# A set-attention block with a gated feed-forward layer: in the last batch, from slot 12 on, products 1024 wide with two value tiles of two banks and three gate tiles of one bank, stage 2's scores copied aside first

## The chip, the cores and the metric

The kernel runs on one core of one Trainium2 chip. The metric is the time of one execution on the device, in microseconds (us); the time before is the median of three executions. TensorE (PE in the profile) multiplies matrices and writes PSUM, which has eight banks of 512 float32 values per partition; VectorE (DVE) and ScalarE (ACT) read PSUM, GpSimd (POOL) does not; SyncE (SP) issues most of the transfers.

## The reference

There are four batches of 12416 tokens of 128 channels, 32 inducing vectors, and a feed-forward layer of width 1536.

```python
def mab(q, kv):
    s = scale * (q @ kv.transpose(0, 2, 1))
    s = s - s.max(-1, keepdims=True)
    a = np.exp(s)
    a /= a.sum(-1, keepdims=True) + 1e-09
    return a @ kv
h = mab(I, x)          # stage 1: 32 inducing vectors attend to the tokens
x = mab(x, h)          # stage 2: every token attends to the 32 rows of h
gate = 1.0 / (1.0 + np.exp(-(x @ w_gate)))
val = x @ w_val
out = gate * val @ w_out
```

## The kernel before

Stage 2's result is never built. The attention weights of a token have only 32 entries, so the kernel multiplies `h` by the two weight matrices once per batch (`hwt`, the tile named `hw`) and obtains value and gate of a token directly from its 32 weights (`a2r`). A matmul for this is 32 rows deep and 512 columns (tokens) wide; which quarter of TensorE's rows it takes follows from the column group `j` and from whether it is a gate (rows 0 or 32) or a value (rows 64 or 96).

The work of the feed-forward layer is cut into *blocks* of 512 tokens, 24 blocks per batch, and one last block of 128 tokens of each batch: 97 blocks. A block has 12 column groups `j` of 128 hidden units (`NJ` = 12). These 12 are done in *steps*: a step of two groups (1024 columns for VectorE and ScalarE), then one of one group (512 columns), and so on, so that a block has four pairs of steps, 776 steps in all. For a step `t`,

- `hidden_mm(st, "v")` fills the value tile and `hidden_mm(st, "g")` the gate tile, by TensorE (line 1012),
- `gate(t)` takes tanh of half the gate from PSUM to `t16`, by ScalarE (line 1031),
- `product(t)` computes (tanh + 1) x value from PSUM to `u16`, by VectorE (line 1044),
- `project` multiplies `u16` by `w_out` and adds up in the accumulator bank `acc`, four matmuls of 128 x 128 per column group, by TensorE (line 1075); at a block's end ScalarE copies the accumulator, halved, to `o32` (line 1093) and SyncE stores it.

PSUM is full: the value and the gate tile of a pair have two banks each (`v2`, `g2`), those of a single one each (`v1`, `g1`), the accumulator has one (`acc`), and one (`m`) serves all else: scores of both stages, sums, the making of `hwt`. Each tag has one buffer, so a tile is filled again only once its last reader is done.

The order of the work is written by hand, and every engine's queue runs in it. The main loop calls, for each step, `product(t)` (which issues the value fills of `t` and the gate fills of `t + 2`), `gate(t + 2)`, and every second step a slot of other work (`beside`) and then `project` with up to three or four column groups. Two steps make one slot. The other work is planned by slot in the dictionary `plan`: `plan_stage2(b, c, score, take, weigh, ...)` puts the scores of 16 tokens' columns at the slots `score` and `score + 1` (TensorE, line 611, eight matmuls each into bank `m`), their copy to `sc` at `take` (ScalarE, line 645), the subtraction of the maximum by GpSimd (`lower`), the exponential at `weigh` (ScalarE, line 671), and sums, scaling and a transposing transfer after it. For the last batch the groups' scores lie at slots 4, 20, 36 and 56 after its first step (`o`).

Of the kernel before, what the change touches and what calls it, by code (L numbers as in the profile page):

```python
# [9 lines left out]
F32 = mybir.dt.float32  # L10
# [7 lines left out]
P = 128  # L18
GC = 16
# [7 lines left out]
def kernel(  # L27
# [34 lines left out]

    ps = ctx.enter_context(tc.tile_pool(name="ps", bufs=1, space=bass.MemoryType.PSUM))

    xv = x.rearrange("b (p j) c -> b p j c", p=P)
    ov = out.rearrange("(b p j) c -> b p j c", b=B, p=P)
# [648 lines left out]
        for j in range(n):  # L717
            a2[(b, c + j)] = (a2r, j)

    def plan_stage2(b, c, score, take, weigh, far=None, soon=False, lag=None):  # L720
# [6 lines left out]
        def room():  # L727
            st["sc"] = s2p.tile([P, GC + NLO, m], F32, tag="sc", name="sc", bufs=1)
# [265 lines left out]
    for i in range(len(blocks)):  # L994
        for j in range(0, NJ, 3):
            steps.append(dict(block=i, j0=j, cnt=2))
            steps.append(dict(block=i, j0=j + 2, cnt=1))
    NST = len(steps)

    def hidden_mm(st, what, halves=False):  # L1000
        pt = ps.tile([P, st["cnt"], 512], F32, tag=f"{what}{st['cnt']}", name=f"{what}_ps")
        pieces, col = [], 0
        for b, c, nb in blocks[st["block"]]:
            pieces += [(k, b, c, nb, col) for k in range(st["cnt"])]
            col += nb * P
        if not halves and st["block"] < len(blocks) - 1:
            pieces.sort(key=lambda p: p[0])
        for k, b, c, nb, col in pieces:
            j = st["j0"] + k
            r = 32 * (j % 2 + (2 if what == "v" else 0))  # L1010
            a2r, o = a2[(b, c)]
            st[what + "end"] = nc.tensor.matmul(  # L1012
                pt[:, k, col : col + nb * P],
                hw[b][r : r + 32, j // 2, :],
                a2r[r : r + 32, o : o + nb, :].rearrange("p j t -> p (j t)"),
                start=True,
                stop=True,
            )
        st[what] = pt

    def gate_fill(t):
        if t < NST:
            hidden_mm(steps[t], "g", t == 0)

    def gate(t):
        if t < NST:
            st = steps[t]
            st["t"] = tp.tile([P, st["cnt"], 512], F16, tag=f"t{st['cnt']}", name="t16")
            cuts = [0, 512] if t else [0, 256, 512]
            for c, e in zip(cuts, cuts[1:]):  # L1030
                st["tanh"] = nc.scalar.activation(  # L1031
                    out=st["t"][:, :, c:e], in_=st["g"][:, :, c:e], func=AF.Tanh, scale=0.5
                )

    def product(t):
        st = steps[t]
        hidden_mm(st, "v")
        if t == 0:
            keep_on(3, "acc")
        gate_fill(t + 2)  # L1040
        st["u"] = up.tile([P, st["cnt"], 512], F16, tag=f"u{st['cnt']}", name="u16")
        cuts = [0, 512] if 0 < t < NST - 1 else [0, 256, 512]
        for c, e in zip(cuts, cuts[1:]):
            u = nc.vector.scalar_tensor_tensor(  # L1044
                out=st["u"][:, :, c:e],
                in0=st["t"][:, :, c:e],
                scalar=1.0,
                in1=st["v"][:, :, c:e],
                op0=ALU.add,
                op1=ALU.mult,  # L1050
            )
            if t == 0 and c == 0:
                turn_b()
        if st["cnt"] == 2 and 4 <= t < NST - 2:

            tc.declare_no_dep(u.ins, st["tanh"].ins, reason="the gate fill of t + 2 waits for it")
            tc.add_manual_dep(
                u.ins, steps[t + 2]["gend"].ins.name, AFTER, reason="tanh, gate fill, product"
            )

    acc = [None]
# [3 lines left out]
    def project(upto, now, room):  # L1065
        while queue and queue[-1][0] < upto and room > 0:
            t, k = queue.pop()
            st = steps[t]
            j = st["j0"] + k
            if j == 0:  # L1070
                acc[0] = [ps.tile([P, BC, C], F32, tag="acc", name="acc_ps")]
                if st["block"] == len(blocks) - 1:
                    acc[0].append(ps.tile([P, BC, C], F32, tag="m", name="acc_ps"))
            for i in range(BC):
                nc.tensor.matmul(  # L1075
                    acc[0][(i // 2) % len(acc[0])][:, i, :],
                    st["u"][:, k, ts(i, P)],
                    wo16[:, NI * (j % 2) + j // 2, :],
                    start=(j == 0 and i in ((0, 2) if len(acc[0]) > 1 else (0,))),
                    stop=(j == NJ - 1),  # L1080
                    skip_group_check=True,
                )
            room -= 1
            if t == NST - 1:
                o32 = op.tile([P, BC, C], F32, tag="o32")
                nc.scalar.mul(out=o32[:, 0:2], in_=acc[0][0][:, 0:2], mul=0.5)
                nc.scalar.dma_start(ov0[:, 0, 0:2, :], o32[:, 0:2])
                nc.vector.tensor_scalar_mul(out=o32[:, 2:4], in0=acc[0][1][:, 2:4], scalar1=0.5)
                nc.sync.dma_start(ov0[:, 0, 2:4, :], o32[:, 2:4])
            elif j == NJ - 1:  # L1090
                block = blocks[st["block"]]
                o32 = op.tile([P, BC, C], F32, tag="o32")
                nc.scalar.mul(out=o32[:], in_=acc[0][0][:], mul=0.5)  # L1093
                b, c, nb = block[0]
                nc.sync.dma_start(ov[b, :, c : c + BC, :], o32[:])
                if now < NST:
                    return


    base = [first_step[(b, 0)] // 2 for b in range(B)]  # L1100
    for b in range(B):
# [6 lines left out]
        for s in range(3 if b == 0 else 2, NG - 1):  # L1108
            k = o + 16 * s - 28
            if b == 0 and s == 4:  # L1110
                k += 1
                plan_stage2(b, groups[s][0], k, k + 1, k + 13)
                continue
            lag = k + 4 if b and more and s == 3 else None
            plan_stage2(b, groups[s][0], k, k + 2, k + (14 if more else 10), lag=lag)
        late = 2 if more and b else 0
        plan_stage2(b, groups[NG - 1][0], o + 56, o + 58, o + 66, far=o + 52 + late)
        if not more:
            continue
        if b == 0:  # L1120
            parts = {
                2: (23, (29, 29, 29)),
# [98 lines left out]
```

## Time and profile before

| | |
|---|---|
| median of 3 executions | 716.75 us (716.66 to 716.96) |
| the profiled execution | 717.17 us |
| its span, first to last instruction | 715.1 us |
| granted TensorE clock | 1.00 |
| VectorE busy | 697.7 us (98%) |
| ScalarE busy | 674.2 us (94%) |
| TensorE busy | 647.6 us (91%) |
| GpSimd busy | 446.7 us (62%) |

A row of the profile names line, engine, operation, tile written <- tiles read, partitions x elements, count, and behind the bar the busy time in us, the mean of one in ns and the idle time ahead of it. A timeline's row begins with its start and its length in us; neighbours of one kind are drawn into one row (`x12`). For a matmul, 32\*128 or 128\*128 is its rows times columns of the array. Rows of one engine may overlap: the next instruction starts before the one ahead of it has delivered.

### The profile page before, as it was taken

The page shows a single profiled execution, that of the slowest core. Times are in us where ns is not written, and L with a number is a line of the kernel's source. Part 1 is how long each engine was busy: PE and PEld are TensorE (multiplying, and loading weights), DVE is VectorE, ACT ScalarE, POOL GpSimd, SP SyncE. Part 2 cuts the span into 40 slices and gives each one's busy share as a digit, 9 for nine tenths or more (in the row PEclk, how much of TensorE's full clock was granted, in tenths as well). Part 3 has the DMA queues.
Part 4 walks back from the last instruction along what each step waited for, and adds up shares of the span by engine and source line. Part 5 has one row for each costly group of instructions (what it writes and reads, how often), then busy time and mean ns, then how long its engine had stood idle before and what let it go on. Part 6 is the DMA issues. An engine that isn't in the chain of part 4 may idle for free.

```text
span 715.1 us, 21664 instructions
## 1 busy us (share of the span) xinstructions
PE 647.6 (91%) x8475; PEld 393.0 (55%) x8475; DVE 697.7 (98%) x850; ACT 674.2 (94%) x1018; POOL 446.7 (62%) x780
## 2 busy tenths in 40 slices
PE   7999899998999999999999989999989889898887
PEld 4555455555555555555555556555555555555555
DVE  4899999999999999999999999999999999999998
ACT  4799999999999999999999999999999999999996
POOL 4568863887558978668656887587737546535100
PEclk9999999999999999999999999999999999999999
DMA  8979864253583264255485132221222123121211
GB/s 172 176 134 181 144 133 95 75 120 87 111 162 77 63 119 107 58 118 109 92 154 107 53 76 77 57 64 46 62 76 60 46 75 61 45 61 46 67 40 47
DMA packets 117111, 65.24 MB, mean 91 GB/s; under 512 B 100208, under 2 KB 101392, under 8 KB 117008
## 3 DMA queue, kind: packets, MB, share of 16 engines
q1 hardware_dynamic: 112320, 49.83, 30.8%
q0 software_dynamic: 4416, 13.90, 10.9%
q8 instruction: 66, 1.08, 0.6%
q14 instruction: 37, 0.30, 0.1%
q10 hardware_dynamic: 272, 0.13, 0.1%
HBM read 27.80 MB, written 25.43 MB: 74 GB/s over the span
## 4 chain that ended last, share of the span: by engine, by line
DVE 48%; issue 20%; PE 17%; ACT 12%; DMA 2%; DVEq 1%; POOL 0%; ACTq 0%; POOLq 0%
DVE u L1044 46%; ACT t L1031 11%; PE acc_ps L1075 8%; PE v_ps L1012 6%; DMA xn<-in_x_dram 2%; PE hp_ps L283 1%; DVE nm L235 1%; DVEq L1044 1%; PE g_ps L1012 1%; POOL xn L82 0%; ACT a1T L248 0%; ACT hwt L470 0%; PE s_ps L223 0%; PE aT_ps L261 0%; PE s_ps L611 0%
## 5 line engine op out<-in xcount | busy, mean ns | idle before, releaser
L1044 DVE SCALAR_TENSOR_TENSOR u<-t,v_ps 128x512 f16<-128x512 f16 (+1 forms) x778 | 674.9, 945 | 1.1 <-ACT t L1031 0.6
L1031 ACT ACTIVATE t<-g_ps 128x512 f16<-128x512 f32 (+1 forms) x777 | 592.3, 820 | 20.6 <-ACT t L1031 12.5
L1012 PE MATMUL v_ps<-a2r,hwt 32*128 32x512 f16 (+1 forms) x1188 | 293.5, 371 | 55.3 <-DVE u L1044 53.9
L1075 PE MATMUL acc_ps<-wo,u 128*128 128x128 f16 x4656 | 327.4, 220 | 0.1
L1075 PEld LDWEIGHTS <-u 128*128 128x128 f16 x4656 | 261.0, 98 | 88.4 <-issue 87.5
L1012 PE MATMUL g_ps<-a2r,hwt 32*128 32x512 f16 (+1 forms) x1188 | 296.6, 377 | 0.0
L1012 PEld LDWEIGHTS <-hwt 32*128 32x128 f16 x2424 | 92.6, 91 | 185.9 <-issue 140.4
L701 POOL TENSOR_TENSOR a2n<-e,rs 128x2048 f16<-128x2048 f16 (+3 forms) x25 | 86.8, 3474 | 5.0 <-DVE rs L690 2.1
L679 POOL TENSOR_TENSOR sum<-e 128x256 f32<-128x256 f16 (+1 forms) x23 | 15.4, 670 | 97.5 <-ACT e L671 97.5
L440 POOL TENSOR_TENSOR near<-sme,minus 128x16 f32<-128x16 f32 (+1 forms) x22 | 65.2, 2963 | 1.6
L1093 ACT ACTIVATE o<-acc_ps 128x512 f32<-128x512 f32 x96 | 58.2, 606 | 0.0
L655 POOL TENSOR_TENSOR rise<-sc 128x256 f32<-128x256 f32 (+1 forms) x22 | 16.2, 738 | 43.4 <-ACT sc L645 43.3
L656 POOL TENSOR_SCALAR rise<-rise 128x256 f32<-128x256 f32 (+6 forms) x110 | 30.1, 273 | 9.6
L659 POOL TENSOR_TENSOR top<-top,rise 128x128 f32<-128x128 f32 (+3 forms) x88 | 28.3, 321 | 7.3
L679 POOL TENSOR_TENSOR sum<-sum 128x128 f32<-128x128 f32 (+3 forms) x92 | 28.3, 307 | 7.2
L655 POOL TENSOR_TENSOR rise<-top 128x128 f32<-128x128 f32 (+3 forms) x88 | 27.2, 309 | 6.9
L662 POOL TENSOR_TENSOR sc<-sc,top 128x512 f32<-128x512 f32 (+1 forms) x22 | 23.9, 1085 | 1.7
L611 PEld LDWEIGHTS <-xT 128*128 128x128 f16 x388 | 13.0, 96 | 11.7 <-issue 11.3
L82 POOL DMA_DIRECT2D xn<-in_x_dram x25 | 14.9, 602 | 6.5 <-DMA xn<-in_x_dram 5.6
L611 PE MATMUL s_ps<-hT,xT 128*128 128x32 f16 x388 | 18.1, 178 | 0.1
L659 POOL TENSOR_TENSOR top<-sc,rise 128x256 f32<-128x256 f32 (+1 forms) x22 | 16.2, 738 | 1.8
L362 POOL TENSOR_TENSOR xT<-xT 128x512 f32<-128x512 f32 (+2 forms) x13 | 12.4, 957 | 4.2 <-ACT xT L345 3.6
(160 smaller groups left out, 281.9 us busy)
## 6 DMA issues: line engine op xcount, KB each, us to landing
out_dram<-o SPq DMA_DIRECT2D x96, 256.0 KB, 2.2
xn<-in_x_dram POOLq DMA_DIRECT2D x19, 512.0 KB, 7.9
xn<-in_x_dram POOLq DMA_DIRECT2D x4, 544.0 KB, 6.2
a2r<-a2n SPq DMA_TRANSPOSE x29, 4.4
xT<-xn SPq DMA_TRANSPOSE x27, 4.3
xn<-in_x_dram POOLq DMA_DIRECT2D x1, 384.0 KB, 15.1
wg<-in_moe_w_gate_dram POOLq DMA_DIRECT2D x1, 384.0 KB, 16.5
wv<-in_moe_w_val_dram POOLq DMA_DIRECT2D x1, 384.0 KB, 16.6
```

The lines of the kernel that those rows point to most:

```text
L440: nc.gpsimd.tensor_tensor(out=near, in0=x, in1=minus, op=ALU.pow)
L611: nc.tensor.matmul(s2[:, j, :], xT[b][:, c + j, :], hT16[b][:], start=(j == 0), stop=whole and j == j1 - 1, skip_group_check=True,)
L655: nc.gpsimd.tensor_tensor(out=r, in0=far, in1=near, op=ALU.subtract)
L656: nc.gpsimd.tensor_scalar(out=r, in0=r, scalar1=BIG, scalar2=0.0, op0=ALU.min, op1=ALU.max)
L659: nc.gpsimd.tensor_tensor(out=top[:, 0:n, 0:w], in0=near, in1=r, op=ALU.add)
L679: nc.gpsimd.tensor_tensor(out=d[:, 0:n, :], in0=src[:, :, 0:w], in1=src[:, :, w : 2 * w], op=ALU.add)
L701: eng.tensor_tensor(out=a2n[:, 0:n, :, :], in0=e.unsqueeze(2).to_broadcast((P, n, 4, m)), in1=rs.unsqueeze(2).unsqueeze(3).to_broadcast((P ...
L1012: st[what + "end"] = nc.tensor.matmul(pt[:, k, col : col + nb * P], hw[b][r : r + 32, j // 2, :], a2r[r : r + 32, o : o + nb, :].rearrange ...
L1031: st["tanh"] = nc.scalar.activation(out=st["t"][:, :, c:e], in_=st["g"][:, :, c:e], func=AF.Tanh, scale=0.5)
L1044: u = nc.vector.scalar_tensor_tensor(out=st["u"][:, :, c:e], in0=st["t"][:, :, c:e], scalar=1.0, in1=st["v"][:, :, c:e], op0=ALU.add, op1= ...
L1075: nc.tensor.matmul(acc[0][(i // 2) % len(acc[0])][:, i, :], st["u"][:, k, ts(i, P)], wo16[:, NI * (j % 2) + j // 2, :], start=(j == 0 and ...
L1093: nc.scalar.mul(out=o32[:], in_=acc[0][0][:], mul=0.5)
```

## The change

The first 600 steps stay as they are, up to slot 12 of the last batch (`T0`). From there on, 22 blocks, the tags `g2`, `g1`, `v1` and `m` are closed, and their five banks are given out anew: a second value tile of two banks (`vw`, beside `v2`) and three gate tiles of one bank (`gw0`, `gw1`, `gw2`). A block then has six steps of two column groups, whose products are all 1024 wide, with value tiles `v2` and `vw` in turn; the gates are filled and put through tanh one column group at a time (`single_fill`, `single_gate`), into a ring of 24 places in the token tile of the batch before (`ring_t`).

Since bank `m` is gone, stage 2's scores of the last four groups of the last batch are computed before slot 12 (at `o - 8`, `o`, `o + 4`, `o + 8`) and copied into the transposed token tile of the batch before; GpSimd's part and all behind it keep their slots (`low`, `weigh`). The loop after `T0` issues per step the product, then twice a column group's projection, with a gate fill and a tanh between; behind a block's store one projection place stays empty.

Matmul work on TensorE around one pair of steps before, within the last batch (`hwt` is the stationary tile of a fill, `u` of a projection):

```order
L1012 LDWEIGHTS hwt
L1012 MATMUL v_ps<-a2r,hwt 128x512
...
L1012 MATMUL g_ps<-a2r,hwt 128x512
L1075 LDWEIGHTS u_14247
L1075 MATMUL acc_ps<-wo_109,u_14247 128x128
...
L1075 LDWEIGHTS u_14255
L1075 MATMUL acc_ps<-wo_109,u_14255 128x128
...
L1012 LDWEIGHTS hwt
L1012 MATMUL v_ps<-a2r,hwt 128x512
```

The left-out rows repeat these: behind the fills of value and gate stand eight projections of a pair and four of a single, and then the fills of the next pair and single, six matmuls, with nothing between them. Now one step of 1024 on TensorE:

```order
L1044 MATMUL v_ps<-a2r,hwt 128x512
...
L1044 MATMUL g_ps<-a2r,hwt 128x512
L1127 LDWEIGHTS u_14175
L1127 MATMUL acc_ps<-wo_112,u_14175 128x128
...
L1044 LDWEIGHTS hwt
L1044 MATMUL g_ps<-a2r,hwt 128x512
L1127 LDWEIGHTS u_14175
L1127 MATMUL acc_ps<-wo_112,u_14175 128x128
...
L1044 MATMUL v_ps<-a2r,hwt 128x512
```

Two value fills and one gate fill stand ahead of four projections, then one gate fill alone and four projections more, then the next step's value fills. Fills stand between projections twice per 1024 columns, where before they did so once per 1536. On ScalarE, one block before and behind it the next:

```order
L1093 ACTIVATE o_14199<-acc_ps 128x512
L1031 ACTIVATE t_14210<-g_ps 128x1024
L1031 ACTIVATE t_14226<-g_ps 128x512
...
L1093 ACTIVATE o_14331<-acc_ps 128x512
L1031 ACTIVATE t_14342<-g_ps 128x1024
```

And now (`xn` is the token tile that holds the ring, `xT` the one that holds the scores):

```order
L1145 ACTIVATE o_12841<-acc_ps 128x512
L1067 ACTIVATE xn_1758<-g_ps 128x512 x7
L684 ACTIVATE e<-xT_3926 128x512
L1067 ACTIVATE xn_1758<-g_ps 128x512 x5
L1145 ACTIVATE o_12973<-acc_ps 128x512
```

Between two output copies stood four tanh of 1024 and four of 512; now there are twelve of 512, and a stage 2 exponential in one of four blocks.

The diff, cut to its core:

```diff
+    class Banks:
+        pools = {}
+        def open(self, stack, name, *tags):
+            pool = stack.enter_context(tc.tile_pool(name=name, bufs=1, space=bass.MemoryType.PSUM))
+            self.pools.update((tag, pool) for tag in tags)
+    ps.open(ctx, "ps", "v2", "acc")
+    ps.open(narrow, "psn", "g2", "g1", "v1", "m")
...
         def room():
+            if low is not None:
+                c0 = (c - NLO) // GC * 9
+                st["sc"] = (
+                    xT[b - 1][:, c0 : c0 + 9, :]
...
-            at(take if lag is None else lag, lower, late=lag is None)
+            at(low or take if lag is None else lag, lower, late=lag is None)
...
+    gates = steps
+    T0 = first_step[(B - 1, 0)] + 2 * 12
+    steps = gates[:T0]
+    singles = []
+    for i in range(gates[T0]["block"], len(blocks)):
+        for j in range(0, NJ, 2):
+            steps.append(dict(block=i, j0=j, cnt=2, bank="vw" if j % 4 else "v2"))
+        singles += [dict(block=i, j0=j, cnt=1, bank=f"gw{j % 3}") for j in range(NJ)]
...
+    def ring_t(i, n):
+        c = i % 24 * BC
+        return xn[B - 2][:, c : c + n * BC, :].rearrange("p (j a) c -> p j (a c)", a=BC)
+    def single_fill(i):
+        if i < len(singles):
+            hidden_mm(singles[i], "g")
+    def single_gate(i):
+        if i < len(singles):
+            nc.scalar.activation(out=ring_t(i, 1), in_=singles[i]["g"][:], func=AF.Tanh, scale=0.5)
...
-        gate_fill(t + 2)
+        if t < T0:
+            gate_fill(t + 2)
+        else:
+            single_fill(2 * (t - T0) + 3)
+            st["t"] = ring_t(2 * (t - T0), 2)
...
-        cuts = [0, 512] if 0 < t < NST - 1 else [0, 256, 512]
+        cuts = [0, 256, 512] if t == 0 else [0, 512] if t < NST - 1 else [0, 384, 512]
...
-                acc[0] = [ps.tile([P, BC, C], F32, tag="acc", name="acc_ps")]
-                if st["block"] == len(blocks) - 1:
-                    acc[0].append(ps.tile([P, BC, C], F32, tag="m", name="acc_ps"))
+                acc[0] = ps.tile([P, BC, C], F32, tag="acc", name="acc_ps")
...
                 if now < NST:
-                    return
+                    return True
+        return False
...
+            if not more:
+                early = o + 4 * (s - 2) - (8 if s == 2 else 4)
+                plan_stage2(b, groups[s][0], early, early + 2, k + 10, low=k + 2)
+                continue
...
+        if not more:
+            plan_stage2(b, groups[NG - 1][0], o + 8, o + 10, o + 66, far=o - 4, low=o + 58)
+            continue
...
-    for t in range(NST):
+    for t in range(T0):
...
+    narrow.close()
+    ps.open(ctx, "psw", "vw", "gw0", "gw1", "gw2")
+    stored = False
+    for t in range(T0, NST):
+        product(t)
+        for i in (3, 4):
+            if stored:
+                stored = False
+            else:
+                stored = project(t - 1, t, 1) or (waiting(t - 1) >= 2 and project(t - 1, t, 1))
+            if i == 3:
+                single_gate(2 * (t - T0) + 3)
+                single_fill(2 * (t - T0) + 4)
+        single_gate(2 * (t - T0) + 4)
+        six, part = divmod(t - T0, 3)
+        for slot, late in ([(0, False)], [(0, True), (1, False)], [(1, True)])[part]:
+            beside(T0 // 2 + 2 * six + slot, late)
```

In the last block the accumulator is one bank instead of two, and the two column groups of the last step are projected piece by piece.

More of the change, by code (lines that the diff above doesn't have):

```diff
@@ L61, with tile @@
     op = ctx.enter_context(tc.tile_pool(name="op", bufs=3))
-    ps = ctx.enter_context(tc.tile_pool(name="ps", bufs=1, space=bass.MemoryType.PSUM))
+    class Banks:
[3 more added lines that the diff above has]
+            self.pools.update((tag, pool) for tag in tags)
+        def tile(self, shape, dtype, tag, name):
+            return self.pools[tag].tile(shape, dtype, tag=tag, name=name)
+    ps = Banks()
+    ps.open(ctx, "ps", "v2", "acc")
+    narrow = ctx.enter_context(ExitStack())
+    ps.open(narrow, "psn", "g2", "g1", "v1", "m")
     xv = x.rearrange("b (p j) c -> b p j c", p=P)
@@ L718, in s2_turn_dma, with plan_stage2 @@
             a2[(b, c + j)] = (a2r, j)
-    def plan_stage2(b, c, score, take, weigh, far=None, soon=False, lag=None):
+    def plan_stage2(b, c, score, take, weigh, far=None, soon=False, lag=None, low=None):
         st = {}
@@ L997 @@
             steps.append(dict(block=i, j0=j + 2, cnt=1))
+    gates = steps
+    T0 = first_step[(B - 1, 0)] + 2 * 12
+    assert gates[T0]["j0"] == 0
+    steps = gates[:T0]
[4 more added lines that the diff above has]
+        singles += [dict(block=i, j0=j, cnt=1, bank=f"gw{j % 3}") for j in range(NJ)]
     NST = len(steps)
     def hidden_mm(st, what, halves=False):
-        pt = ps.tile([P, st["cnt"], 512], F32, tag=f"{what}{st['cnt']}", name=f"{what}_ps")
+        tag = st.get("bank") or f"{what}{st['cnt']}"
+        pt = ps.tile([P, st["cnt"], 512], F32, tag=tag, name=f"{what}_ps")
         pieces, col = [], 0
@@ L1021, in gate_fill @@
     def gate_fill(t):
-        if t < NST:
-            hidden_mm(steps[t], "g", t == 0)
+        if t < T0 + 2:
+            hidden_mm(gates[t], "g", t == 0)
+    def ring_t(i, n):
[7 more added lines that the diff above has]
+            nc.scalar.activation(out=ring_t(i, 1), in_=singles[i]["g"][:], func=AF.Tanh, scale=0.5)
     def gate(t):
-        if t < NST:
-            st = steps[t]
-            st["t"] = tp.tile([P, st["cnt"], 512], F16, tag=f"t{st['cnt']}", name="t16")
+        if t < T0 + 2:
+            st = gates[t]
+            st["t"] = ring_t(2 * (t - T0), st["cnt"]) if t >= T0 else tp.tile([P, st["cnt"], 512], F16, tag=f"t{st['cnt']}", name="t16")
             cuts = [0, 512] if t else [0, 256, 512]
@@ L1053, in product @@
                 turn_b()
-        if st["cnt"] == 2 and 4 <= t < NST - 2:
+        if st["cnt"] == 2 and 4 <= t < T0:
             tc.declare_no_dep(u.ins, st["tanh"].ins, reason="the gate fill of t + 2 waits for it")
             tc.add_manual_dep(
-                u.ins, steps[t + 2]["gend"].ins.name, AFTER, reason="tanh, gate fill, product"
+                u.ins, gates[t + 2]["gend"].ins.name, AFTER, reason="tanh, gate fill, product"
             )
@@ L1070, in project @@
             if j == 0:
-                acc[0] = [ps.tile([P, BC, C], F32, tag="acc", name="acc_ps")]
-                if st["block"] == len(blocks) - 1:
-                    acc[0].append(ps.tile([P, BC, C], F32, tag="m", name="acc_ps"))
[L1074 to L1080, printed above, removed]
+                acc[0] = ps.tile([P, BC, C], F32, tag="acc", name="acc_ps")
+            todo = [(k, i) for i in range(BC)]
+            if t == NST - 1:
+                k, _ = queue.pop()[1], None
+                j = st["j0"] + k
+                todo = [(n, i) for n in range(2) for i in range(BC - 1)] + [(n, BC - 1) for n in range(2)]
+            for n, i in todo:
+                e = st["j0"] + n
+                nc.tensor.matmul(
+                    acc[0][:, i, :],
+                    st["u"][:, n, ts(i, P)],
+                    wo16[:, NI * (e % 2) + e // 2, :],
+                    start=(e == 0 and i == 0),
+                    stop=(e == NJ - 1),
                     skip_group_check=True,
@@ L1092, in project @@
                 o32 = op.tile([P, BC, C], F32, tag="o32")
-                nc.scalar.mul(out=o32[:], in_=acc[0][0][:], mul=0.5)
+                nc.scalar.mul(out=o32[:], in_=acc[0][:], mul=0.5)
                 b, c, nb = block[0]
@@ L1113 @@
                 continue
-            lag = k + 4 if b and more and s == 3 else None
-            plan_stage2(b, groups[s][0], k, k + 2, k + (14 if more else 10), lag=lag)
-        late = 2 if more and b else 0
+            if not more:
+                early = o + 4 * (s - 2) - (8 if s == 2 else 4)
+                plan_stage2(b, groups[s][0], early, early + 2, k + 10, low=k + 2)
+                continue
+            lag = k + 4 if b and s == 3 else None
+            plan_stage2(b, groups[s][0], k, k + 2, k + 14, lag=lag)
+        if not more:
+            plan_stage2(b, groups[NG - 1][0], o + 8, o + 10, o + 66, far=o - 4, low=o + 58)
+            continue
+        late = 2 if b else 0
         plan_stage2(b, groups[NG - 1][0], o + 56, o + 58, o + 66, far=o + 52 + late)
-        if not more:
-            continue
         if b == 0:
```

9 lines of the change are left out of this document (7 added, 2 removed).

## The prediction

> **What bounds the kernel now.** The page's busy line comes first, then its chain of waits, then the busy table of a stretch of the last batch that the change rewrites (from 556 to 697 us; columns PE, PEld, DVE, ACT, POOL), then the list of what TensorE waited for there.
>
> ```profile
> PE 647.6 (91%) x8475; PEld 393.0 (55%) x8475; DVE 697.7 (98%) x850; ACT 674.2 (94%) x1018; POOL 446.7 (62%) x780
> ...
> DVE 48%; issue 20%; PE 17%; ACT 12%; DMA 2%; DVEq 1%; POOL 0%; ACTq 0%; POOLq 0%
> ...
> 556.00:697.00 141.00, 126.25 (x1514) 75.22 (x1512) 140.92 (x165) 133.46 (x192) 58.76 (x95) 1.00 0.20 54
> ...
> PE v_ps L1012 <- DVE u L1044: 15.7, 79, 0.2
> ```
>
> VectorE is busy in 140.92 of 141 us and leads the chain. TensorE waits for it about once per pair of steps, 0.2 us each (15.7 us in 79 waits between 553 and 705 us). So VectorE sets the pace, and TensorE follows with a small reserve. ScalarE's 133 us look as if it were nearly full too, but the times of neighbouring rows overlap, so for all three engines I read the distance from one start to the next. VectorE, three looks at one place:
>
> ```profile
> 642.70 1.81 DVE L1044 SCALAR_TENSOR_TENSOR u<-t,v_ps 128x512 f16<-128x512 f16 x2
> 643.30 1.21 DVE L1044 SCALAR_TENSOR_TENSOR u<-t,v_ps 128x1024 f16<-128x1024 f16 x1
> 644.43 0.68 DVE L1044 SCALAR_TENSOR_TENSOR u<-t,v_ps 128x512 f16<-128x512 f16 x1
> ```
>
> A 512-wide product starts at 642.70, the 1024-wide one 0.60 later, the next 512-wide one 1.13 after that: a pair of steps (1536 columns) takes 1.73, although the two durations add up to 1.89. A block of 12 columns of 512 is four such pairs, 6.92 us. ScalarE:
>
> ```profile
> 642.52 0.59 ACT L1031 ACTIVATE t<-g_ps 128x512 f16<-128x512 f32 x1
> 643.00 0.60 ACT L1093 ACTIVATE o<-acc_ps 128x512 f32<-128x512 f32 x1
> 643.48 1.04 ACT L1031 ACTIVATE t<-g_ps 128x1024 f16<-128x1024 f32 x1
> ```
>
> 512-wide operations of ScalarE follow each other at 0.48. TensorE, in a stretch in which a stage 2 score falls in:
>
> ```profile
> 572.32 0.38 PE L1012 MATMUL v_ps<-a2r,hwt 32*128 32x512 f16 x1
> 572.32 0.39 PE L1012 MATMUL g_ps<-a2r,hwt 32*128 32x512 f16 x1
> 572.64 0.84 PE L1075 MATMUL acc_ps<-wo,u 128*128 128x128 f16 x12
> 573.42 0.39 PE L1012 MATMUL v_ps<-a2r,hwt 32*128 32x512 f16 x2
> 573.43 0.39 PE L1012 MATMUL g_ps<-a2r,hwt 32*128 32x512 f16 x2
> 573.75 0.37 PE L611 MATMUL s_ps<-hT,xT 128*128 128x32 f16 x8
> 574.05 0.39 PE L1012 MATMUL v_ps<-a2r,hwt 32*128 32x512 f16 x1
> 574.05 0.38 PE L1012 MATMUL g_ps<-a2r,hwt 32*128 32x512 f16 x1
> 574.37 0.84 PE L1075 MATMUL acc_ps<-wo,u 128*128 128x128 f16 x12
> 575.15 0.39 PE L1012 MATMUL v_ps<-a2r,hwt 32*128 32x512 f16 x2
> ...
> L1075 PE MATMUL acc_ps<-wo,u x1104: 219/219/230, 553.6 to 711.3; 128*128 128x128 f16 x184
> ```
>
> Fills of value and gate that stand together, two or four, start within 0.01 us of each other. Whatever comes behind them starts 0.32 later, be it projections (572.32 to 572.64, 574.05 to 574.37) or scores (573.43 to 573.75), and behind two fills as behind four. Twelve projections last 0.84 with a last one of 0.22, so they start 0.056 apart; the fills behind them start 0.78 after the first, 0.16 after the last. So **a group of fills costs a flat price**: from one group's start to the next, with twelve projections between, it is 1.10, of which 12 x 0.056 = 0.67 are the projections and 0.43 the group, with one fill in it or four. That is the number on which this change turns.
>
> **The change, part by part.** *VectorE.* Six 1024-wide products replace four pairs: 6 x 1.13 = 6.78 in place of 6.92 per block. From slot 12 on there are 22 blocks: 22 x 0.14 = 3.1 us less, if VectorE goes on setting the pace.
>
> *ScalarE.* Twelve 512-wide gates and one output copy: 13 x 0.48 = 6.24 per block, and one exponential per four blocks, some 0.5. This is 6.4 and stays below VectorE. The four score copies, 0.48 each, go ahead of slot 12, where ScalarE has spare time.
>
> *TensorE.* The same matmuls, in another order. Before, a pair of steps had one place at which fills stand between projections: four fills, then the two of the single step, then twelve projections. Now every step of 1024 has two: two value fills and a gate fill, four projections, one gate fill alone, four projections. Where a block is stored, the slot behind it projects nothing and two groups run together, so a block has 11 groups and 48 projections: 11 x 0.43 + 48 x 0.056 = 4.73 + 2.69 = **7.4 us**. This is above VectorE's 6.78 and above today's 6.92. No work of VectorE or ScalarE hides it; TensorE becomes what the others wait for.
>
> No row shows a gate fill alone between projections. From below it could cost no more than its issue, 0.06 as a projection; from above a group's 0.43. I take 0.43, since two fills cost what four do, and since the switch to the scores costs the same 0.32. The printed forms say why this is likely: fills are 32\*128, projections and scores 128\*128, so each group is a change of form and back. The Trainium skill, "TensorEngine Tiling (Array Packing)", section "Key Properties", says that a change of tiling mode, not merely of tile, drains TensorE; by that rule a lone fill pays what a group pays and the block is the 7.4 above, and without it, at the lower bound, 7.4 - 5 x 0.37 = 5.6. Those rows agree with the rule as far as they reach.
>
> *The block's end.* There is one accumulator bank. The next block's first projection needs the output copy to be over, and the copy needs the last projection:
>
> ```profile
> 641.72 0.39 PE L1012 MATMUL g_ps<-a2r,hwt 32*128 32x512 f16 x1
> 642.03 0.84 PE L1075 MATMUL acc_ps<-wo,u 128*128 128x128 f16 x12
> 642.84 0.39 PE L1012 MATMUL v_ps<-a2r,hwt 32*128 32x512 f16 x2
> 643.44 0.37 PE L1012 MATMUL v_ps<-a2r,hwt 32*128 32x512 f16 x1 [0.20 <-DVE u L1044]
> 643.44 0.39 PE L1012 MATMUL g_ps<-a2r,hwt 32*128 32x512 f16 x1
> 643.76 0.23 PE L1075 MATMUL acc_ps<-wo,u 128*128 128x128 f16 x1
> ```
>
> The block's last projection starts at 642.03 + 0.62 = 642.65, the copy at 643.00 (above), 0.35 later. It lasts 0.60. From a release to the waiting fill it is 0.06 (the product of 642.70 ends 0.68 later, at 643.38; the fill starts at 643.44). Together 1.01 from the last projection to the next one that may start. Today 1.11 pass there anyway (642.65 to 643.76), so nothing is seen of it. After the change only one group stands between, 0.16 + 0.32 = 0.48, and TensorE is held in order for up to 0.53; if ScalarE took the copy the moment the projection ends, 0.22 in place of 0.35, it is 0.40. I take 0.5: behind it are queued TensorE's four projections and the next value and gate fills.
>
> A second wait follows. The gate behind the copy on ScalarE starts 0.48 after it, 0.83 after the last projection, and lasts 0.59; with 0.06 its bank is free at 1.48. The third bank's next fill wants it after the four projections, at 1.01 + 0.17 + 0.16 = 1.34. That is 0.14 more; nothing less is excluded, so 0 to 0.14, and I take 0.14, by the same rows. Per block: 7.4 + 0.5 + 0.14 = **8.05**, 1.13 more than 6.92.
>
> *What is moved ahead.* The scores are eight matmuls per slot, copied by ScalarE at 0.48; in the stretch above they lie between the two fill groups, and the single's fill comes 0.63 after the pair's (573.42 to 574.05), against 0.60 where there is no score (642.84 to 643.44). So nine such slots cost at most 9 x 0.03 = 0.3 ahead of slot 12. The subtraction on POOL, the exponentials and the transposes on SP's queue keep their slots, with later sources waiting in memory. When the banks are cut anew at slot 12, the first fills wait once for the old tiles, at most a step, 1.1. For both together I take 0.5, from 0 to 1.4.
>
> *The end.*
>
> ```profile
> 709.35 0.38 PE L1012 MATMUL v_ps<-a2r,hwt 32*128 32x128 f16 x4 [0.20 <-DVE u L1044]
> ...
> 711.31 0.38 ACT L1086 ACTIVATE o<-acc_ps 128x256 f32<-128x256 f32 x1 [2.27 <-PE acc_ps L1075]
> 711.52 0.42 DVE L1088 TENSOR_SCALAR o<-acc_ps 128x256 f32<-128x256 f32 x1 [0.38 <-PE acc_ps L1075]
> ```
>
> From the last value fills to the copies it is 2.0 to 2.2 us. The new last step has one product of 1024 in two pieces, 1.1 plus one start, behind a VectorE that is no longer behind; the two copies now read one bank, and if one waits for the other that is 0.4. I take no change, -0.4 to +0.4.
>
> Sum: 22 x 1.13 + 0.5 = 25.4 us on the profiled execution's 715.1 us span, 740.5. That execution took 717.17 with what lies around the span, 0.4 over the median of 716.75; I add the difference to the median: 742.1, so **742 us**, 3.5% slower.
>
> **Rivals.**
>
> *TensorE bound, without the waits at the block's end (728).* If ScalarE and the three gate banks happen to be in time, a block is 7.4: 22 x 0.48 + 0.5 = 11 us, 728. For it speaks that the copy's 0.35 was measured behind a busy ScalarE. Against it that the copy alone, 0.60, is longer than the 0.48 between.
>
> *TensorE bound, with longer switches (749).* In the stretch of 642 the fills come 0.19 behind the last projection (642.65 to 642.84), not 0.16. If that is how it always is with a wait on the fill, a block has 11 x 0.03 = 0.33 more, 22 x 0.33 = 7 us: 749. Against it: the product of 1024 ahead of the one at 642.70 started 1.13 earlier, lasts 1.21 and so ends at 642.78; the fills come 0.06 behind that end, which is a wait for VectorE that the new pace would not have.
>
> *VectorE still bound, the gain as counted (714).* The mechanism: the lone gate fill does not stop the stream of projections, since it uses a quarter of the rows, and its price lies near 0.06. Then TensorE's block, with 0.5 at its end, is 6.1 and VectorE's 6.78 decides: 716.75 - 3.1 + 0.5, about 714. It decides from a lone fill under (6.92 - 7.4 - 0.5 + 5 x 0.43) / 5 = 0.23 on, half of what every group in the rows costs. Against it stand both kinds of switch shown, after two fills and after four.
>
> That the steps are not 1024 wide after all is excluded by the order of instructions.
>
> **How the numbers follow.** TensorE bound with the waits 0.63 (its own range 737 to 746, from 0.40 to 0.53 and 0 to 0.14 per block and the two ends); without them 0.15; longer switches 0.12; VectorE bound 0.06; a mixture near today's time 0.04. Range 728 to 748: it takes in the case without waits and leaves out the gain and the longest switches. Below 0.2%, 1.4 us, a measurement of this kernel cannot be told from no change. Slower by more 0.92; within it 0.03; faster 0.05, nearly all from VectorE bound.
>
> **What would show it.** Right: after slot 12 the list of waits has VectorE waiting for `v_ps` fills, and the waits of TensorE for `u` are gone; a 1024-wide product starts every 1.3 us and more, not every 1.13; a lone gate fill is followed by projections 0.32 later; output copies stand 8 us apart; at each block's end TensorE waits about 0.5 for the copy. Wrong: products back to back at 1.13 there, or a lone fill after which projections start within 0.2.

## The result

The changed kernel takes 739.5 us (median of 4 runs, 739.2 to 742.0) against 716.7 for the kernel before: 1.032 times as long, with a 95% interval of 1.0303 to 1.0337. The prediction was 742 us, 3.5% slower, with a range of 728 to 748. The profiled execution has a span of 737.3 us in place of 715.1, 22.2 more.

The page's busy line and its chain of waits, for the changed kernel:

```profile
PE 679.0 (92%) x8475; PEld 397.6 (54%) x8475; DVE 706.1 (96%) x806; ACT 690.4 (94%) x1105; POOL 447.6 (61%) x780
...
PE 37%; DVE 34%; issue 14%; ACT 13%; DMA 2%; DVEq 0%; POOL 0%; ACTq 0%; POOLq 0%
```

VectorE led the chain with 48%; now TensorE has 37%, though it is not much busier by its share of the span (92%). The list of waits in the rewritten stretch, 575 to 730 us, says more:

```profile
PE acc_ps L1127 <- ACT o L1145: 7.1, 20, 0.4
ACT o L1145 <- PE acc_ps L1127: 6.8, 20, 0.3
DVE u L1092 <- PE g_ps L1044: 5.6, 19, 0.3
```

TensorE's waits for VectorE (15.7 us before) are gone. In their place stand 20 waits of TensorE for the output copy, one per block, and 20 of the copy for TensorE's last projection: at each block's end the copy waits for the projections, and then the projections wait for the copy. VectorE now waits for TensorE. The list names the gate fill (`g_ps`), not the value fill that the prediction named, but the two are issued in one group, as the rows at 642.83 below show. The timeline shows how TensorE's time runs within a block, from the end of one block's projections on:

```profile
640.08 0.39 PE L1044 MATMUL v_ps<-a2r,hwt 32*128 32x512 f16 x2
640.09 0.39 PE L1044 MATMUL g_ps<-a2r,hwt 32*128 32x512 f16 x2
640.83 0.38 PE L1127 MATMUL acc_ps<-wo,u 128*128 128x128 f16 x4 [0.36 <-ACT o L1145]
641.15 0.39 PE L1044 MATMUL v_ps<-a2r,hwt 32*128 32x512 f16 x2
641.32 0.37 PE L1044 MATMUL g_ps<-a2r,hwt 32*128 32x512 f16 x1
641.62 0.62 PE L1127 MATMUL acc_ps<-wo,u 128*128 128x128 f16 x8
642.18 0.39 PE L1044 MATMUL g_ps<-a2r,hwt 32*128 32x512 f16 x1
642.50 0.40 PE L1127 MATMUL acc_ps<-wo,u 128*128 128x128 f16 x4
642.83 0.39 PE L1044 MATMUL v_ps<-a2r,hwt 32*128 32x512 f16 x2
642.83 0.38 PE L1044 MATMUL g_ps<-a2r,hwt 32*128 32x512 f16 x1
643.15 0.40 PE L1127 MATMUL acc_ps<-wo,u 128*128 128x128 f16 x4
643.48 0.39 PE L1044 MATMUL g_ps<-a2r,hwt 32*128 32x512 f16 x1
643.80 0.40 PE L1127 MATMUL acc_ps<-wo,u 128*128 128x128 f16 x4
644.12 0.39 PE L1044 MATMUL v_ps<-a2r,hwt 32*128 32x512 f16 x2
```

A group of three fills and four projections take 642.83 to 643.48, 0.65 us; the fill that stands alone and its four projections take 643.48 to 644.12, 0.64. One fill costs what three cost. A step of 1024 is their sum, 1.3, and VectorE, which would take 1.13, follows it:

```profile
643.31 1.22 DVE L1092 SCALAR_TENSOR_TENSOR u<-xn,v_ps 128x1024 f16<-128x1024 f16 x1 [0.30 <-PE g_ps L1044]
644.61 1.22 DVE L1092 SCALAR_TENSOR_TENSOR u<-xn,v_ps 128x1024 f16<-128x1024 f16 x1
645.91 1.22 DVE L1092 SCALAR_TENSOR_TENSOR u<-xn,v_ps 128x1024 f16<-128x1024 f16 x1
```

At the block's end, the projections behind the merged group come 0.75 after its fills (640.08 to 640.83), where 0.32 is the rule: a wait of 0.43 for the copy. Behind these projections the gate fill comes 0.17 after the value fills of its own group (641.15 to 641.32). It waits for its bank, which was filled three gates earlier; the tanh that reads it stands behind the output copy and ends at 641.27. The output copies give the block's length over a long stretch (first and last start, and their count):

```profile
L1145 ACT ACTIVATE o<-acc_ps x16: 597/597/598, 576.6 to 695.8; 128x512 f32<-128x512 f32 x16
```

15 blocks in 119.2 us, 7.95 each, where it was 6.92. 21 blocks of 1.03 more make 21.6; the other 0.6 lies in the first steps behind slot 12. From the last full output copy to the end it is 9.6 us, as before (9.7), so the end costs nothing.

### The profile page after: what moved, and what is told of

Its sections match the earlier page's. It is cut to its first block, busy times and chain, and to the rows that moved or that the text cites. A ratio compares the mean times of both kernels' runs of the same rounds, so it can differ in the third digit from the quotient of the medians.

```text
span 737.3 us, 21607 instructions
## 1 busy us (share of the span) xinstructions
PE 679.0 (92%) x8475; PEld 397.6 (54%) x8475; DVE 706.1 (96%) x806; ACT 690.4 (94%) x1105; POOL 447.6 (61%) x780
## 4 chain that ended last, share of the span: by engine, by line
PE 37%; DVE 34%; issue 14%; ACT 13%; DMA 2%; DVEq 0%; POOL 0%; ACTq 0%; POOLq 0%
DVE u L1092 32%; PE acc_ps L1127 18%; PE v_ps L1044 10%; ACT t L1075 10%; PE g_ps L1044 6%; ACT o L1145 2%; DMA xn<-in_x_dram 2%; PE hp_ps L296 1%; DVE nm L248 1%; DVEq L1092 0%; POOL xn L95 0%; ACT a1T L261 0%; ACT hwt L483 0%; PE s_ps L236 0%; PE aT_ps L274 0%
## 5 line engine op out<-in xcount | busy, mean ns | idle before, releaser
L1092 DVE SCALAR_TENSOR_TENSOR u<-t,v_ps 128x512 f16<-128x512 f16 x601 | 522.3, 947 | 1.0 <-ACT t L1075 0.6
L1075 ACT ACTIVATE t<-g_ps 128x512 f16<-128x512 f32 x601 | 458.4, 820 | 11.5 <-ACT t L1075 4.7
L1127 PE MATMUL acc_ps<-wo,u 128*128 128x128 f16 x4656 | 353.5, 220 | 8.2 <-ACT o L1145 7.8
L1044 PE MATMUL g_ps<-a2r,hwt 32*128 32x512 f16 (+1 forms) x1188 | 321.1, 377 | 0.3 <-DVE u L1092 0.2
L1044 PE MATMUL v_ps<-a2r,hwt 32*128 32x512 f16 (+1 forms) x1188 | 277.6, 373 | 38.0 <-DVE u L1092 36.8
L1044 PEld LDWEIGHTS <-hwt 32*128 32x128 f16 x2424 | 95.1, 91 | 159.3 <-issue 97.8
L1092 DVE SCALAR_TENSOR_TENSOR u<-xn,v_ps 128x1024 f16<-128x1024 f16 (+1 forms) x133 | 161.1, 1213 | 14.0 <-PE g_ps L1044 6.3
L1067 ACT ACTIVATE xn<-g_ps 128x512 f16<-128x512 f32 x261 | 145.2, 604 | 8.1 <-PE g_ps L1044 1.3
L668 POOL TENSOR_TENSOR rise<-sc 128x256 f32<-128x256 f32 (+1 forms) x18 | 13.3, 737 | 21.5 <-ACT sc L658 21.4
L675 POOL TENSOR_TENSOR sc<-sc,top 128x512 f32<-128x512 f32 (+1 forms) x18 | 19.6, 1086 | 1.4
## 6 DMA issues: line engine op xcount, KB each, us to landing
wv<-in_moe_w_val_dram POOLq DMA_DIRECT2D x1, 384.0 KB, 16.5
```

Source lines behind the costliest of these rows:

```text
L668: nc.gpsimd.tensor_tensor(out=r, in0=far, in1=near, op=ALU.subtract)
L1044: st[what + "end"] = nc.tensor.matmul(pt[:, k, col : col + nb * P], hw[b][r : r + 32, j // 2, :], a2r[r : r + 32, o : o + nb, :].rearrange ...
L1067: nc.scalar.activation(out=ring_t(i, 1), in_=singles[i]["g"][:], func=AF.Tanh, scale=0.5)
L1075: st["tanh"] = nc.scalar.activation(out=st["t"][:, :, c:e], in_=st["g"][:, :, c:e], func=AF.Tanh, scale=0.5)
L1092: u = nc.vector.scalar_tensor_tensor(out=st["u"][:, :, c:e], in0=st["t"][:, :, c:e], scalar=1.0, in1=st["v"][:, :, c:e], op0=ALU.add, op1= ...
L1127: nc.tensor.matmul(acc[0][:, i, :], st["u"][:, n, ts(i, P)], wo16[:, NI * (e % 2) + e // 2, :], start=(e == 0 and i == 0), stop=(e == NJ - 1),
```

## The experiments

The theory was that every group of fills costs TensorE a flat 0.42 us, whatever is in it, so that the five lone fills of a block, each a group of its own, make TensorE the bound. Rivals were that the narrow gates or their new place slow the products (B), that the waits at a block's end are most of the loss (C), that the moved scores cost something (B'), and that any lone 512-wide matmul would cost as much (D).

**Both gate fills beside the value fills.** In the changed kernel:

```diff
             single_fill(2 * (t - T0) + 3)
+            single_fill(2 * (t - T0) + 4)
...
                 single_gate(2 * (t - T0) + 3)
-                single_fill(2 * (t - T0) + 4)
```

> The changed kernel with one edit: both gate fills of a step stand beside its two value fills, so that no gate fill stands alone between projections; widths, tiles, tanh and ring are as in the change. Theory A (every group of fills costs TensorE 0.43 us, whatever is in it): a block has 6 groups in place of 11, TensorE's block is 6 x 0.43 + 48 x 0.056 = 5.3 us, below VectorE's 6.79, VectorE sets the pace again with a product every 1.13 us, and the 22 blocks give back 22 x (7.94 - 6.79) = 25 us: 714 us. Theory B (the narrow gates, their ring in the token tile or the three banks slow the products, in whatever order): unchanged at about 739. Theory C (the waits at a block's end are most of it): 13 x 0.5 less at most, about 730 to 739.

Measured 716.0 us, 0.9988 of the kernel before (0.9978 to 0.9999). The place of the five lone fills per block is all that differs from the change, and it gives back 23.5 us, all of the 22.8 that the change had cost and a little more. B falls: widths, tiles, ring and copies are those of the change. C falls as a cause of its own: TensorE still waits for the output copy here, 3.8 us in 17 waits between 575 and 700 us, and no time is lost by it. The busy table of two blocks, with PE, DVE and ACT in the first, third and fourth place, shows what the expectation missed:

```profile
615.63:622.88 7.25, 6.54 (x75) 3.56 (x75) 7.25 (x8) 7.10 (x14) 1.99 (x6) 1.00 0.09 36
622.88:629.63 6.75, 6.37 (x75) 3.47 (x72) 6.49 (x7) 6.59 (x13) 6.34 (x6) 1.00 0.11 41
```

The stretches run from one output copy's start to the next. Most blocks take 6.75 us, near the 6.79 forecast, but three of them, with a stage 2 exponential among ScalarE's instructions (14 in place of 13), take 7.25. Rows of another such block, whose exponential starts at 592.28:

```profile
593.45 0.37 PE L1044 MATMUL g_ps<-a2r,hwt 32*128 32x512 f16 x1 [0.24 <-ACT xn L1067]
...
598.58 1.22 DVE L1093 SCALAR_TENSOR_TENSOR u<-xn,v_ps 128x1024 f16<-128x1024 f16 x1 [0.26 <-PE g_ps L1044]
```

A gate fill waits 0.24 for the tanh that stands behind the exponential. The chain of waits in this trace leads from the exponential over this fill to the value fills of a later step, for which the product at 598.58 waits 0.26. From start to start VectorE loses 0.34 at each of the three exponentials, 1.0 us in all, and 1.3 in the first two blocks behind slot 12, one of which has an exponential too. That is more than two thirds of the gain of 3 us that the wide products have to give.

**The scores alone moved ahead**, in the kernel before:

```diff
...
+                early = o + 4 * (s - 2) - (8 if s == 2 else 4)
+                plan_stage2(b, groups[s][0], early, early + 2, k + 10, low=k + 2)
...
+            plan_stage2(b, groups[NG - 1][0], o + 8, o + 10, o + 66, far=o - 4, low=o + 58)
```

> The kernel before, with only stage 2's scores of the last batch ahead of slot 12 and copied aside; pairs and singles, banks and order of fills are those of before. Theory A: nothing that can be told from 716.7 (at most 0.3 us). Theory B': the crowded slots ahead of slot 12 cost VectorE 1 us or more: 717.7 to 718.5.

Measured 716.6 us, a ratio of 1.0000 (0.9991 to 1.0008): the moved scores cost nothing, and B' falls.

**A lone fill in the kernel before.** The single step's gate fill, with its tanh, is put behind the first four projections, from slot 12 of the last batch on:

```diff
-        gate_fill(t + 2)
+        if t < 600 or t % 2 == 0:
+            gate_fill(t + 2)
...
+            room = 3 if waiting(t - 1) <= 3 else 4
+            if t >= 600:
+                project(t - 1, t, 1)
+                room -= 1
+                gate_fill(t + 2)
+                gate(t + 2)
             project(t - 1, t, room)
```

> The kernel before, with one edit from slot 12 of the last batch on: the gate fill of the single step (512 wide) no longer stands beside the single's value fill but alone behind the first four of the twelve projections; widths and banks are those of before. Theory A: one more group per pair of steps. TensorE's pair is 0.40 + 0.32 + 0.62 + 0.16 = 1.50 today and 1.93 then, above VectorE's 1.73: a block of 7.7, with some wait for the output copy 7.85, and 22 x 0.8 to 0.95 = 18 to 21 us: 734 to 738. Rival (a lone fill of a quarter of the rows lets the projections run on, under 0.23 us): 716 to 717.

Measured 733.8 us, 1.0234 of before (1.022 to 1.0248), just under the expected 734 to 738. No width, no bank and no copy is changed here; one fill out of its group costs 17 us over 22 blocks. TensorE's timeline of one pair of steps:

```profile
640.90 0.39 PE L1012 MATMUL v_ps<-a2r,hwt 32*128 32x512 f16 x2
640.91 0.39 PE L1012 MATMUL g_ps<-a2r,hwt 32*128 32x512 f16 x2
641.34 0.37 PE L1012 MATMUL v_ps<-a2r,hwt 32*128 32x512 f16 x1
641.64 0.40 PE L1076 MATMUL acc_ps<-wo,u 128*128 128x128 f16 x4
641.97 0.39 PE L1012 MATMUL g_ps<-a2r,hwt 32*128 32x512 f16 x1
642.29 0.62 PE L1076 MATMUL acc_ps<-wo,u 128*128 128x128 f16 x8
642.84 0.39 PE L1012 MATMUL v_ps<-a2r,hwt 32*128 32x512 f16 x2
```

A pair takes 1.94 (640.90 to 642.84), where 1.93 was worked out; the four projections and the lone fill stand 0.65 apart from the next (641.64 to 642.29).

**A shorter copy.** The changed kernel copies and stores one quarter of each block and leaves out the rest:

```diff
-                nc.scalar.mul(out=o32[:], in_=acc[0][:], mul=0.5)
+                some = BC if st["block"] < 75 else 1
+                nc.scalar.mul(out=o32[:, 0:some], in_=acc[0][:, 0:some], mul=0.5)
...
-                nc.sync.dma_start(ov[b, :, c : c + BC, :], o32[:])
+                nc.sync.dma_start(ov[b, :, c : c + some, :], o32[:, 0:some])
```

> The changed kernel, where the output copy of the blocks after slot 12 (but the last block) copies and stores one quarter of the block's 512 tokens; the other three quarters of these blocks' output are left out. The copy lasts some 0.28 in place of 0.60. Theory A: the waits at the block's end shrink from 0.43 for the accumulator and 0.17 for the third gate bank to 0.1 and 0, the 11 groups stay: block 7.4 to 7.45, 728 to 730. Theory C (the waits explain the loss): below 722. A theory without these waits: 739.

Measured 732.5 us, 1.0215 of before (1.0201 to 1.0229). It gives back 7 us of the 23, less than expected (728 to 730). Around a block's end:

```profile
644.77 0.39 PE L1044 MATMUL g_ps<-a2r,hwt 32*128 32x512 f16 x2
645.20 0.38 PE L1127 MATMUL acc_ps<-wo,u 128*128 128x128 f16 x4
645.51 0.39 PE L1044 MATMUL v_ps<-a2r,hwt 32*128 32x512 f16 x2
645.69 0.37 PE L1044 MATMUL g_ps<-a2r,hwt 32*128 32x512 f16 x1
```

The output copies of the same kernel, by their tile:

```profile
L1146 ACT ACTIVATE o<-acc_ps x17: 277/277/277, 576.3 to 698.2; 128x128 f32<-128x128 f32 x17
```

At this block's end the projections come 0.43 after the fills (644.77 to 645.20), so the wait for the accumulator falls to 0.43 - 0.32 = 0.11. The wait for the third gate bank stays at 0.18 (645.51 to 645.69). The shorter copy lets the gate behind it start earlier, and TensorE's projections by as much, so the distance between them is the same. A block is 121.9 / 16 = 7.62, which is 0.32 or 0.33 less, and 22 times this is the whole gain of 7 us.

C, as the whole of the loss, falls: 16 us are left. But the waits are no small part of it. In the changed kernel they are 0.43 + 0.17 = 0.60 of the 1.03 by which a block is longer, and 0.29 of them are still here. The lone fills make TensorE the bound: without any of these waits its block would be 7.95 - 0.60 = 7.35, above the 6.92 of before. Only because of that do the waits come on top; in the grouped kernel they cost nothing.

**A lone matmul without a change of form.** In the changed kernel the lone gate fill becomes a matmul of 128 rows: `full_fill` multiplies 512 columns of `xT` by a 128 x 128 tile of `wo16`, into the same bank.

```diff
-                single_fill(2 * (t - T0) + 4)
+                full_fill(2 * (t - T0) + 4)
```

> The changed kernel, where the gate fill that stands alone between projections is replaced by one matmul of the projections' own form (128 rows x 128 columns, 512 columns streamed) into the same bank from other tiles; the gates of every second column group are thus computed from something else, all counts, widths and waits stay. Theory A (the price is the change of form and back, as read from 0.15 ahead of and 0.32 behind every group of fills): without the change of form the lone matmul costs its stream alone, at most 0.22 in place of 0.42; five of them save 1.0 us per block, a block is 6.9 to 7.0 us, 716 to 719 us. Rival D (the price is that of any lone matmul of 512 columns, its length and its wait for the bank, in whatever form): about 739.

Measured 717.1 us, 1.0002 of before (0.9993 to 1.0012), within the expected 716 to 719. D falls. TensorE's timeline:

```profile
641.44 0.40 PE L1141 MATMUL acc_ps<-wo,u 128*128 128x128 f16 x4
641.67 0.38 PE L1070 MATMUL g_ps<-xT,wo 128*128 128x512 f16 x1
641.89 0.39 PE L1141 MATMUL acc_ps<-wo,u 128*128 128x128 f16 x4
642.21 0.39 PE L1044 MATMUL v_ps<-a2r,hwt 32*128 32x512 f16 x2
```

The lone matmul starts 0.23 after the first of four projections, so 0.05 after the last (four last 0.40, one 0.22), like a projection, and the next projection 0.22 after it. The form 32\*128 has 0.15 ahead and 0.32 behind. Same width, same bank, same waits: the change of form and back costs 0.2 us. The Trainium skill, "TensorEngine Tiling (Array Packing)", section "Key Properties", says that a change of tiling mode drains TensorE; this run agrees and gives the size, 0.1 on the way in and 0.1 on the way out. That it is a drain which takes this time, no row shows by itself.

This edit alone leaves a rival: any matmul of 32 rows might hold up what follows it, in whatever form. The last block of the kernel before speaks against it. Its fills are 128 wide, and in a single step the value fills all take one quarter of the rows:

```profile
704.14 0.21 PE L1012 MATMUL v_ps<-a2r,hwt 32*128 32x128 f16 x1
704.16 0.21 PE L1012 MATMUL g_ps<-a2r,hwt 32*128 32x128 f16 x1
704.19 0.21 PE L1012 MATMUL v_ps<-a2r,hwt 32*128 32x128 f16 x1
704.22 0.21 PE L1012 MATMUL g_ps<-a2r,hwt 32*128 32x128 f16 x1
704.37 0.84 PE L1075 MATMUL acc_ps<-wo,u 128*128 128x128 f16 x12
```

One value fill follows the other after 0.05 to 0.06, as one projection does another. The projections come 0.15 after the last fill, 0.1 more, where the form changes.

**Every second step grouped.**

```diff
+            if t % 2 == 0:
+                single_fill(2 * (t - T0) + 4)
...
+                if t % 2:
                     single_fill(2 * (t - T0) + 4)
```

> The changed kernel, where in every second step both gate fills stand beside the value fills: 9 groups of fills per block in place of 11, still above VectorE's pace. Theory A (a flat price of 0.42 per group): 2 x 0.42 less per block, 7.94 - 0.84 = 7.1 us, with up to 0.2 more if the third gate bank comes late in the grouped steps: 721 to 725 us. If the loss were the waits at the block's end, or the width of the gates: 739.

Measured 723.0 us, 1.0086 of before (1.0072 to 1.01), the middle of what was expected (721 to 725). Nine groups in place of eleven take away 16.5 us: the loss grows with the count of groups. Most output copies are 7.10 apart, as worked out, and 7.50 to 7.53 in the three blocks with an exponential.

**Can the wide products pay?** In the grouped kernel, the exponential in two halves:

```diff
...
+            at(weigh, lambda: exp_part(0, GC // 2))
+            at(weigh, lambda: exp_part(GC // 2, n), late=True)
```

> The grouped kernel, where stage 2's exponential of the last groups after slot 12 is issued as two halves in consecutive steps. In the grouped kernel three of the blocks took 7.25 us in place of 6.75, those with an exponential on ScalarE. Theory: ScalarE is nearly full there (13 x 0.48 + 0.52 of 6.75), and 0.52 in one piece holds up the gate banks; in two pieces of 0.3 the reserve of a step takes it up: those blocks fall to 6.75 to 6.9, 1 to 1.5 us less than the grouped kernel, 714.5 to 715. Rival (ScalarE's sum decides, not the piece): 716 or a little more.

Measured 715.6 us, 0.9986 of before (0.9977 to 0.9995). That is 0.4 us less than in one piece, where 1 to 1.5 was expected, and by the two ratios (0.9986 and 0.9988) the times cannot be told apart. ScalarE's rows show the halves, each with 0.3 us to the next start:

```profile
590.74 0.46 ACT L801 ACTIVATE e<-xT 128x256 f16<-128x256 f32 x1
591.04 1.14 ACT L1078 ACTIVATE xn<-g_ps 128x512 f16<-128x512 f32 x2
592.00 0.48 ACT L801 ACTIVATE e<-xT 128x256 f16<-128x256 f32 x1
592.31 2.63 ACT L1078 ACTIVATE xn<-g_ps 128x512 f16<-128x512 f32 x5
```

In the traces the halving does act: from start to start VectorE loses 0.18 to 0.19 at an exponential in place of 0.34, and such a block takes 7.10 in place of 7.25.

Then the halves were set further apart, and the three gate tiles were given the freed banks in another order:

```diff
...
-            at(weigh, lambda: exp_part(GC // 2, n), late=True)
+            at(weigh + 1, lambda: exp_part(GC // 2, n), late=True)
...
-    ps.open(ctx, "psw", "vw", "gw0", "gw1", "gw2")
+    ps.open(ctx, "psw", "vw", "gw1", "gw2", "gw0")
```

> The kernel with grouped fills and halved exponentials, with two edits: the second half of an exponential stands two steps behind the first, not one, and the three gate tiles take the freed banks in another order, so that the first gate fill behind slot 12 lies in a bank that has long been free. Theory: the blocks with an exponential, 7.10 us there, fall toward 6.75 (3 x 0.35 = 1.0 us at most), and the first steps behind slot 12, which lose about 1.3 us to the old tiles' readers, lose 0.2 to 0.5 less: 714.0 to 715.4. Rival (ScalarE's sum decides): 715.5, as before.

Measured 715.7 us, 0.9984 of before (0.9975 to 0.9993): no gain by either edit, where 714.0 to 715.4 was expected. The blocks with an exponential take 7.10 as before, so the distance of the halves is not what costs. Why the halves still cost this much is not settled. All three grouped kernels lie below the kernel before, by 0.9 to 1.2 us. Their intervals end below 1, that of the first barely, but the gain is under the 0.2% that the prediction took as the limit.

## Why the prediction was right

*TensorE becomes the bound, by the number of groups.* Right, and shown in three ways: fewer groups with nothing else changed (6 groups 716.0, 9 groups 723.0, 11 groups 739.5), one more group in the kernel before (733.8), and the lone matmul without a change of form (717.1). The price was taken as 0.43 from a stretch where it stood for two and four fills; by the block of the changed kernel it is (7.95 - 0.43 - 0.17 - 48 x 0.056) / 11 = 0.42.

*A lone fill pays a group's price.* This was chosen between 0.06 and 0.43, and is 0.42: 0.64 for the fill and its four projections, less 4 x 0.056.

*The waits at the block's end.* Right in place and kind. The accumulator's wait is 0.43, forecast 0.5. The term that was mis-sized is the start of the copy behind the last projection: 0.35 after the last projection was read at a place where ScalarE was busy; in the changed kernel the last projection starts at 639.93, from the row below, and the copy at 640.19, 0.26 later.

```profile
639.82 0.33 PE L1127 MATMUL acc_ps<-wo,u 128*128 128x128 f16 x3
...
640.19 0.60 ACT L1145 ACTIVATE o<-acc_ps 128x512 f32<-128x512 f32 x1 [0.34 <-PE acc_ps L1127]
```

The wait for the third gate bank is 0.17, forecast 0.14. The block is 7.95, forecast 8.05: 0.07 less by the copy, 0.05 less by the groups and projections (7.35 in place of 7.4), 0.03 more by the gate bank. 22 times this 0.1 is most of the 2.5 us by which the forecast was high. The 737 to 746 given as the own range of this case does not follow from the terms named with it; they add up to 736 to 744.

*The rival without these waits (728)* is out, since the rows show the waits. Its time was about right for a kernel without them: the short copy leaves 0.29 of them per block and takes 732.5, and 22 x 0.29 = 6.4 less is 726. *The rival with longer switches (749)*: the 0.19 ahead of the fills was VectorE's, as argued; where nothing is waited for, it is 0.15, in the changed kernel at every change from projections to fills between 575 and 700 us. *VectorE still bound (714)* needed, by the prediction's sum, a lone fill under 0.23. That sum sets TensorE against 6.92; against VectorE's new pace of 6.78 the same terms give 0.21. The kernel whose lone matmul costs 0.22 took 717.1, with output copies 6.91 apart. The grouped kernel, which VectorE bounds in most blocks, did not reach 714 either, since the exponentials and the first blocks take back 2.3 of the 3 us.

*What is moved ahead* costs nothing (716.6 against 716.9), within the 0 to 0.3 of its term. The first steps behind slot 12 cost 0.6, inside the 0 to 1.4 taken for both.

*VectorE's saving* of 0.14 per block is there where VectorE decides: in the grouped kernel products follow each other after 1.13, six in 6.79, in place of 6.92.

## What to carry to other kernels

Count the places at which TensorE changes between forms of matmul, not the matmuls: here each change and back was 0.2 us on top of the stream, and a fill that lies beside others of other rows was free. An engine that waits a little has a reserve, and a new order of the same work can use it up: look at a step's start-to-start times on every engine before narrowing one tile to widen another. Where one accumulator bank is refilled, compare two times: the copy's way from the last write to the free bank, and the work that lies between. Here the first was longer, and once TensorE was the bound the difference was added to every block.

## What the hardware showed that was not expected

A shorter copy took the accumulator's wait away but left the gate bank's wait at 0.18 us, since both sides of that wait are released by the same copy. And the value fills of a pair and the lone value fill of the next step, with no projection between them, stand 0.44 apart (640.90 to 641.34 in the kernel with a lone fill), 0.12 more than projections have to wait behind fills. The row looks like TensorE's own pace, but VectorE's product that reads the lone fill's bank ends just ahead of it:

```profile
640.61 0.68 DVE L1045 SCALAR_TENSOR_TENSOR u<-t,v_ps 128x512 f16<-128x512 f16 x1
```

It ends at 640.61 + 0.68 = 641.29, and the fill starts 0.05 after, about the 0.06 from a release to a waiting fill in the kernel before. So this reads as a wait for the bank; no run tells how close the fill would come without it.
